# Turning q, k and x by crossbar transposes instead of TensorE in five of eight half batches

## The chip, the cores and the metric

The kernel runs on one core of a Trainium2 chip. Times are device microseconds of one execution; the median of several runs is quoted. A profile is one more execution, with a span a little shorter than the time (233.5 us of 235.3 for the kernel before).

## The reference

Attention with a window of 96 positions, 8 global positions and a linear bias, then a feed-forward layer with a squared ReLU. Shapes: 4 batches, 8 heads, 768 positions, head size 64; model width 512, inner width 2048.

```python
def _attn_ref(q, k, v, n_global, n_local):
    B, H, S, D = q.shape
    scores = np.matmul(q, k.transpose(0, 1, 3, 2)) / np.sqrt(D)
    # keep: key position < n_global, or 0 <= query - key < n_local; bias: -slope[h] * distance
    ...
    a = np.exp(scores - max); a = a / (sum(a) + 1e-09)
    return np.matmul(a, v)

def _moe_ref(x, w_in, w_out):
    h = np.maximum(x @ w_in, 0.0)
    return h * h @ w_out
```

## The kernel before

The work is cut into eight half batches (hb 0 to 7) of 384 rows. While the feed-forward layers of one half batch run on TensorE, the attention of the next is woven in between. Per half batch and pair of heads (four pairs) the attention does this: **turn** q and k (transposes, so that the head size lies on the partitions), **score**, exponential on ScalarE, weighing with a mask on VectorE, **attend** (multiply with v), normalise, and turn the result into **x**, the input of layer 1. Two small copies serve the global positions: `kb` (keys) and `vb` (values, the "fix-up").

```python
def fix_v(x):                                   # the value fix-up
    t0, t1 = tiles_before(x)
    def emit(e):
        v_, vb = x.bt.v, x.bt.vb
        d0, d1 = t0 - 1, t1 - 1
        copy(e, vb[GR:GR * 2, d0:d1], v_[GR:GR * 2, t0:t1])
        copy(e, vb[2 * GR:P, d0:d1], v_[2 * GR:P, t0:t1])
        copy(e, vb[0:GR, d0:d1], v_[0:GR, 0:1].to_broadcast([GR, t1 - t0, H, D + 1]))
    n = t1 - t0
    costs = {"POOL": 0.6 + 2.1 * n} if x.hb > 1 else {"DVE": 0.2 + 0.65 * n}
    x.vb_op = plan.add(costs, emit, x.v_in)

def turn(x, a):                                 # six TensorE transposes, two evacuations, kb
    def emit(e):
        state["ps"] = trp = ps_att.tile([P, 2, HT, P], FP16, name="trp", tag="att")
        for i, st in enumerate((x.sq, x.sk)):
            for t in range(HT):
                nc.tensor.transpose(out=trp[:, i, t, :], in_=st[:, t, 2 * a:2 * a + 2, :],
                                    identity=ident)
    ...
    ops = [evac(0), evac(1)]                    # {"ACT": 0.39, "DVE": 0.31} each
    ...
    x.qk_ops[a] = ops + [plan.add(costs, fix_k, [ops[1]])]

def to_x(x, a):                                 # three transposes, one evacuation
    ...
    job = plan.pe(3 * 0.056, emit, [norm], [att])
    x.x_ops[a] = plan.after(job, {"ACT": 0.39, "DVE": 0.31}, lambda e: copy(
        e, x.xt[:, a, :], st["trx"].rearrange("p t c -> p (t c)")))
```

The order in each engine's queue comes from a schedule computed while the kernel is built: every piece has an estimated cost and a list of what it needs, and goes into its engine's queue where this model says that it can start. On the chip each engine works through its queue in that order, and waits at an instruction whose data are not there (in the changed kernel's profile VectorE stood 2.2 us at one copy in this way). So a piece that the model believes ready too early makes everything behind it wait.

The softmax here doesn't subtract the row's maximum and nothing guards it: scores larger than these inputs give would overflow.

## Time and profile before

| | before |
|---|---|
| time, median of the first 3 runs (range) | 236.13 us (235.42 to 236.17) |
| span of the profile | 233.5 us |
| busy: TensorE, VectorE, ScalarE, GpSimd | 221.1, 126.0, 139.1, 86.2 us |
| half-batch period, mean of five | 26.2 us |

The prediction reads the views that bound the kernel. Here are three groups of instructions from the page of the kernel before that the change removes or moves; the columns are line, engine, operation, destination and source, count, then busy us and mean ns of one, then the idle time before them and who ended it.

```profile
L362 PE MATMUL trp<-ident,sk 128*128 128x128 f16 x84 | 10.0, 226 | 1.5 <-DMA sk<-in_k_dram 1.5
...
L189 ACT COPY qk<-trp 128x384 f16<-128x384 f16 (+1 forms) x43 | 19.9, 506 | 11.4 <-DVE qk L191 10.4
...
L191 POOL COPY vb<-v 32x520 f16<-32x520 f16 (+3 forms) x18 | 19.3, 1070 | 19.1 <-DMA v<-in_v_dram 18.5
```

The second line is an evacuation of turned q or k from PSUM. The third is the value fix-up on GpSimd: about 1 us a copy, and GpSimd waited 18.5 us for v to land before such copies.

### The profile page before, as it was taken

The page shows a single profiled execution, that of the slowest core. Times are in us where ns is not written, and L with a number is a line of the kernel's source. Part 1 is how long each engine was busy: PE and PEld are TensorE (multiplying, and loading weights), DVE is VectorE, ACT ScalarE, POOL GpSimd, SP SyncE. Part 2 cuts the span into 40 slices and gives each one's busy share as a digit, 9 for nine tenths or more (in the row PEclk, how much of TensorE's full clock was granted, in tenths as well). Part 3 has the DMA queues.
Part 4 walks back from the last instruction along what each step waited for, and adds up shares of the span by engine and source line. Part 5 has one row for each costly group of instructions (what it writes and reads, how often), then busy time and mean ns, then how long its engine had stood idle before and what let it go on. Part 6 is the DMA issues. An engine that isn't in the chain of part 4 may idle for free.

```text
span 233.5 us, 5024 instructions
## 1 busy us (share of the span) xinstructions
PE 221.1 (95%) x2023; PEld 133.8 (57%) x2023; DVE 126.0 (54%) x340; ACT 139.1 (60%) x319; POOL 86.2 (37%) x100
## 2 busy tenths in 40 slices
PE   7675999999999999999999999999999999999993
PEld 6553689654555566556655565556655565556541
DVE  5395799441376279425864279325863279323300
ACT  4693797671564598328961598328961598327521
POOL 8948723894457307670292107560000000000000
PEclk9999799999999999999999999999999999999999
DMA  8999999999159907951099107941002100111012
GB/s 149 168 194 155 200 206 193 156 149 108 45 77 164 148 0 50 162 87 46 0 120 171 49 3 51 162 82 45 3 1 93 45 4 0 48 45 45 0 48 90
DMA packets 82583, 20.77 MB, mean 89 GB/s; under 512 B 75392, under 2 KB 79488, under 8 KB 82560
## 3 DMA queue, kind: packets, MB, share of 16 engines
q0 software_dynamic: 74944, 13.11, 74.5%
q1 hardware_dynamic: 6576, 7.08, 9.1%
q10 hardware_dynamic: 1040, 0.26, 0.5%
q8 instruction: 16, 0.26, 0.5%
q14 instruction: 7, 0.06, 0.1%
HBM read 27.26 MB, written 6.29 MB: 144 GB/s over the span
## 4 chain that ended last, share of the span: by engine, by line
PE 88%; POOL 5%; DMA 4%; DVE 0%; issue 0%; ACT 0%; POOLq 0%
PE hps L508 37%; PE yps L556 36%; PE sp L409 5%; PE trp L362 4%; DMA sk<-in_k_dram 4%; PE av L464 4%; PE trx L488 2%; POOL sq L279 2%; POOL v L279 1%; POOL sk L279 1%; POOL w_in_sb L327 1%; ACT y L189 0%; DVE ident L226 0%; DVE qk L191 0%; POOL dist L220 0%
## 5 line engine op out<-in xcount | busy, mean ns | idle before, releaser
L508 PE MATMUL hps<-xt,w_in_sb 128*128 128x384 f16 (+2 forms) x576 | 93.8, 311 | 0.2 <-DMA w_in_sb<-in_moe_w_in_dram 0.2
L556 PE MATMUL yps<-w_out_sb,h 128*128 128x512 f16 x384 | 91.9, 379 | 0.0
L508 PEld LDWEIGHTS <-w_in_sb 128*128 128x128 f16 x576 | 51.4, 99 | 27.7 <-DMA w_in_sb<-in_moe_w_in_dram 0.4
L532 ACT ACTIVATE hr<-hps 128x384 f16<-128x384 f32 (+1 forms) x109 | 56.3, 517 | 12.0 <-PE hps L508 9.8
L543 DVE TENSOR_TENSOR h<-hr 128x768 f16<-128x768 f16 (+1 forms) x68 | 36.8, 541 | 38.0 <-ACT hr L532 36.9
L556 PEld LDWEIGHTS <-h 128*128 128x128 f16 x384 | 34.5, 98 | 33.6
L424 ACT ACTIVATE ex<-sp 128x384 f16<-128x384 f32 x112 | 44.4, 510 | 4.2 <-PE sp L409 4.1
L189 ACT COPY y<-yps 128x512 f32<-128x512 f32 x22 | 12.9, 585 | 55.1 <-PE yps L556 55.1
L279 POOL DMA_DIRECT2D sq<-in_q_dram x23 | 20.8, 914 | 38.0 <-PE trp L362 36.5
L189 ACT COPY qk<-trp 128x384 f16<-128x384 f16 (+1 forms) x43 | 19.9, 506 | 11.4 <-DVE qk L191 10.4
L191 POOL COPY vb<-v 32x520 f16<-32x520 f16 (+3 forms) x18 | 19.3, 1070 | 19.1 <-DMA v<-in_v_dram 18.5
L279 POOL DMA_DIRECT2D v<-in_v_dram x24 | 21.4, 918 | 7.3 <-DMA w_out_sb<-in_moe_w_out_dram 3.3
L279 POOL DMA_DIRECT2D sk<-in_k_dram x21 | 18.6, 908 | 5.9 <-DMA w_out_sb<-in_moe_w_out_dram 3.1
L440 DVE TENSOR_TENSOR phat<-ex,mask 128x768 f16<-128x768 f16 x32 | 16.4, 553 | 5.4 <-ACT ex L424 5.1
L191 DVE COPY qk<-trp 128x384 f16<-128x384 f16 (+1 forms) x19 | 6.9, 365 | 17.5 <-PE trp L362 13.4
L473 DVE TENSOR_TENSOR tm<-av,rec 128x384 f16<-128x384 f32 x28 | 15.6, 557 | 1.0
L464 PEld LDWEIGHTS <-phat 128*128 128x128 f16 x312 | 13.2, 98 | 4.8
L464 PE MATMUL av<-v,phat 128*128 128x65 f16 x192 | 13.2, 193 | 0.0
L436 DVE TENSOR_TENSOR phat<-ex,mask 128x768 f16<-128x768 f16 (+1 forms) x24 | 10.7, 486 | 3.6 <-ACT ex L424 3.5
L464 PE MATMUL av<-vb,phat 128*128 128x65 f16 x120 | 12.1, 193 | 0.0
L191 DVE COPY kb<-qk 128x96 f16<-128x96 f16 (+4 forms) x58 | 10.2, 222 | 3.5 <-ACT qk L189 2.0
L362 PE MATMUL trp<-ident,sk 128*128 128x128 f16 x84 | 10.0, 226 | 1.5 <-DMA sk<-in_k_dram 1.5
(59 smaller groups left out, 154.8 us busy)
## 6 DMA issues: line engine op xcount, KB each, us to landing
out_dram<-y SPq DMA_DIRECT2D x24, 256.0 KB, 2.0
v<-in_v_dram POOLq DMA_DIRECT2D x24, 128.0 KB, 6.3
sq<-in_q_dram POOLq DMA_DIRECT2D x23, 128.0 KB, 5.8
sk<-in_k_dram POOLq DMA_DIRECT2D x21, 128.0 KB, 5.9
w_in_sb<-in_moe_w_in_dram POOLq DMA_DIRECT2D x4, 512.0 KB, 9.0
w_out_sb<-in_moe_w_out_dram POOLq DMA_DIRECT2D x4, 512.0 KB, 14.3
rk<-in_k_dram SPq DMA_DIRECT2D x2, 256.0 KB, 6.2
rk<-in_k_dram ACTq DMA_DIRECT2D x1, 256.0 KB, 4.6
```

What stands on the lines that cost most here:

```text
L189: nc.scalar.copy(out=out, in_=in_)
L191: eng(e).tensor_copy(out=out, in_=in_)
L279: nc.gpsimd.dma_start(out=dst, in_=src[x.b, :, r0 + t * P:r0 + (t + 1) * P, :] .rearrange("h p d -> p h d"))
L362: nc.tensor.transpose(out=trp[:, i, t, :], in_=st[:, t, 2 * a:2 * a + 2, :], identity=ident)
L424: nc.scalar.activation(out=st["ex", g][:, h, 0:n], in_=st[g][h][:, 0:n], func=AF.Exp, scale=scale)
L440: eng(e).tensor_tensor(out=phat[:, :, c0:c0 + n].rearrange("p e (i c) -> p e i c", c=P), in0=ex[:, :, 0:n].rearrange("p e (i c) -> p e i c ...
L464: nc.tensor.matmul(av[:, h, j, :], lhsT=phat[:, h, c * P:(c + 1) * P], rhs=rhs, start=n == 0, stop=n == len(mine) - 1)
L473: nc.vector.tensor_tensor(out=st["tm"].rearrange("p t e d -> p e t d"), in0=av[:, :, :, 0:D], in1=rec[:, :, :, None].to_broadcast([P, 2, H ...
L508: nc.tensor.matmul(st["ps"][:, i * n:(i + 1) * n], lhsT=w_in_sb[:, kk, m * P:(m + 1) * P], rhs=x.xt[:, kk, c0:c1], start=kk == 0, stop=kk ...
L532: nc.scalar.activation(out=o, in_=i, func=AF.Relu)
L543: eng(e).tensor_tensor(out=x.h2[:, m0:m0 + width, c0:c1], in0=hr, in1=hr, op=ALU.mult)
L556: nc.tensor.matmul(st["ps"], lhsT=x.h2[:, m, j * P:(j + 1) * P], rhs=w_out_sb[:, m, :], start=m == 0, stop=m == NFT - 1)
```

## The change

For half batches 3 to 7 q and k are transposed by two DMA transposes (crossbar) from SBUF to SBUF, and x by four. TensorE's transposes and the PSUM evacuations of these half batches go. q and k are turned as soon as loads and the sync queue allow. The value fix-up goes to VectorE, one tile at a time. The layout of `qk` and the places of the attention pieces change to suit. The core, with cuts:

```diff
-        bt.qk = qk_p.tile([P, 2, NPAIR, S], FP16, name="qk", tag="qk")
+        bt.qk = qk_p.tile([P, 2, NT, NPAIR, P], FP16, name="qk", tag="qk")
...
-            return plan.load(0.62, emit, vbefore if name == "v" else before)
+            return plan.load(0.9, emit, vbefore if name == "v" else before)
...
+        x.vb_ops = []
+        for t in range(t0, t1):
+            def emit(e, t=t):
+                copy(e, vb[GR:GR * 2, t - 1], v_[GR:GR * 2, t])
+                copy(e, vb[2 * GR:P, t - 1], v_[2 * GR:P, t])
+                copy(e, vb[0:GR, t - 1], v_[0:GR, 0])
+            x.vb_ops.append(plan.add({"DVE": 0.75}, emit, x.v_in))
...
+    def turn_by_dma(x):
+        ts = slice(x.half * HT, (x.half + 1) * HT)
+        late = list(halves[x.hb - 2].x_ops.values()) if x.hb > 3 else []
+        for i, (name, loads) in enumerate((("sk", x.k_in), ("sq", x.q_in))):
+            def emit(e, i=i, name=name):
+                nc.sync.dma_start_transpose(
+                    out=x.bt.qk[:, 1 - i, ts].rearrange("p t a c -> p (t a) c"),
+                    in_=getattr(x, name).rearrange("p t h d -> p (t h d)"))
+            op = plan.add({"SP": 1.7}, emit, [*loads, x.bt.op, *late])
+            op.lag = 2.5
+            x.turned.append(op)
+        for a in range(NPAIR):
+            x.qk_ops[a] = x.turned + [plan.add(*fix_k(x, a), x.turned[:1])]
...
+    def to_x_by_dma(x, a):
+            nc.sync.dma_start_transpose(
+                out=x.xt[:, a, :].rearrange("p (t c) -> p t c", c=P),
+                in_=st["tm"].rearrange("p t e d -> p (t e d)"))
+        x.x_ops[a] = plan.add({"SP": 1.2}, emit, [norm])
+        x.x_ops[a].lag = 2.5
...
+        early = x.hb > 2
+        for a in range(NPAIR):
+            at = 0.04 + 0.16 * a if early else 0.1 + 0.17 * a
+            jobs.append((at, lambda a=a: score(x, a)))
+            jobs.append((at + 0.17, lambda a=a: attend(x, a)))
+            if early:
+                jobs.append((at + 0.17, lambda a=a: to_x_by_dma(x, a)))
+            else:
+                jobs.append((0.04 * a, lambda a=a: turn(x, a)))
+                jobs.append((at + 0.3, lambda a=a: to_x(x, a)))
```

Six y buffers instead of three, and stores placed by the schedule as pieces of the sync queue, come with it.

More of the change, by code (lines that the diff above doesn't have):

```diff
@@ L176 @@
     h_p = ctx.enter_context(tc.tile_pool(name="hp", bufs=2))
-    y_p = ctx.enter_context(tc.tile_pool(name="yp", bufs=3))
+    y_p = ctx.enter_context(tc.tile_pool(name="yp", bufs=6))
     ps_big = ctx.enter_context(tc.tile_pool(name="ps_big", bufs=6, space=bass.MemoryType.PSUM))
@@ L269, in list_loads @@
         prev = halves[x.hb - 2] if x.hb >= 2 else None
-        before = [prev.turned[-1]] if prev else []
+        before = (prev.turned if prev else []) + (halves[x.hb - 1].turned if x.hb > 3 else [])
         vbefore = [halves[x.hb - x.half - 3].attended[-1]] if x.hb >= 4 else []
@@ L292, in list_loads @@
         else:
-            raw = {n: stage_p.tile([P, HT, H, D], FP32, name=n, tag=n, bufs=1)
-                   for n in ("rq", "rk")}
+            raw = {n: stage_p.tile([P, ts, H, D], FP32, name=n, tag=n, bufs=1)
+                   for n, ts in (("rq", 1), ("rk", HT))}
             x.q_in, x.k_in, x.v_in = [], [], []
@@ L342, in fix_v, with fix_k @@
         t0, t1 = tiles_before(x)
-        def emit(e):
-            v_, vb = x.bt.v, x.bt.vb
-            d0, d1 = t0 - 1, t1 - 1
-            copy(e, vb[GR:GR * 2, d0:d1], v_[GR:GR * 2, t0:t1])
-            copy(e, vb[2 * GR:P, d0:d1], v_[2 * GR:P, t0:t1])
-            copy(e, vb[0:GR, d0:d1], v_[0:GR, 0:1].to_broadcast([GR, t1 - t0, H, D + 1]))
-        n = t1 - t0
-        costs = {"POOL": 0.6 + 2.1 * n} if x.hb > 1 else {"DVE": 0.2 + 0.65 * n}
-        x.vb_op = plan.add(costs, emit, x.v_in)
+        x.vb_ops = []
+        for t in range(t0, t1):
+            def emit(e, t=t):
+                v_, vb = x.bt.v, x.bt.vb
+                copy(e, vb[GR:GR * 2, t - 1], v_[GR:GR * 2, t])
+                copy(e, vb[2 * GR:P, t - 1], v_[2 * GR:P, t])
+                copy(e, vb[0:GR, t - 1], v_[0:GR, 0])
+            x.vb_ops.append(plan.add({"DVE": 0.75}, emit, x.v_in))
+    def fix_k(x, a):
+        t0, t1 = tiles_before(x)
+        def emit(e):
+            kt = x.bt.qk[:, 1, :, a, :]
+            copy(e, x.bt.kb[:, a, t0 - 1:t1 - 1, GR:P], kt[:, t0:t1, GR:P])
+            copy(e, x.bt.kb[:, a, t0 - 1:t1 - 1, 0:GR],
+                 kt[:, 0:1, 0:GR].to_broadcast([P, t1 - t0, GR]))
+        return {"DVE": 0.2 + 0.08 * (t1 - t0)}, emit
     def turn(x, a):
@@ L367, in emit @@
             def emit(e):
-                copy(e, x.bt.qk[:, i, a, x.half * HALF:(x.half + 1) * HALF],
-                     state["ps"][:, i].rearrange("p t c -> p (t c)"))
+                copy(e, x.bt.qk[:, i, x.half * HT:(x.half + 1) * HT, a, :], state["ps"][:, i])
             return plan.after(job, {"ACT": 0.39, "DVE": 0.31}, emit)
         ops = [evac(0), evac(1)]
-        t0, t1 = tiles_before(x)
-        def fix_k(e):
-            kt = x.bt.qk[:, 1, a, :].rearrange("p (t c) -> p t c", c=P)
-            copy(e, x.bt.kb[:, a, t0 - 1:t1 - 1, GR:P], kt[:, t0:t1, GR:P])
-            copy(e, x.bt.kb[:, a, t0 - 1:t1 - 1, 0:GR],
-                 kt[:, 0:1, 0:GR].to_broadcast([P, t1 - t0, GR]))
-        n = t1 - t0
-        costs = {"DVE": 0.2 + 0.08 * n}
-        if x.hb == 0:
-            costs["POOL"] = 0.5 + 0.17 * n
-        x.turned.append(job)
-        x.qk_ops[a] = ops + [plan.add(costs, fix_k, [ops[1]])]
+        x.turned.append(job)
+        x.qk_ops[a] = ops + [plan.add(*fix_k(x, a), [ops[1]])]
+    def turn_by_dma(x):
[11 more added lines that the diff above has]
+            x.qk_ops[a] = x.turned + [plan.add(*fix_k(x, a), x.turned[:1])]
     GROUPS = {
@@ L407, in emit @@
                         lhsT = (bt.kb[rows, a, r - 2, :] if before and r > 1
-                                else bt.qk[rows, 1, a, (r - before) * P:(r - before + 1) * P])
+                                else bt.qk[rows, 1, r - before, a, :])
                         nc.tensor.matmul(pair[h][:, i * P:(i + 1) * P], lhsT=lhsT,
-                                         rhs=bt.qk[rows, 0, a, r * P:(r + 1) * P],
+                                         rhs=bt.qk[rows, 0, r, a, :],
                                          start=True, stop=True)
@@ L465, in emit @@
                                          rhs=rhs, start=n == 0, stop=n == len(mine) - 1)
-        job = plan.pe(0.0305 * 2 * len(where), emit, weighs + [x.vb_op] + x.v_in, [att])
+        job = plan.pe(0.0305 * 2 * len(where), emit, weighs + x.vb_ops + x.v_in, [att])
         def norm(e):
@@ L492, in to_x, with emit @@
             e, x.xt[:, a, :], st["trx"].rearrange("p t c -> p (t c)")))
+    def to_x_by_dma(x, a):
+        st, norm = x.tm[a]
+        def emit(e):
+            if x.xt is None:
+                x.xt = h_p.tile([P, NCT, HALF], FP16, name="xt", tag="xt")
+            nc.sync.dma_start_transpose(
[3 more added lines that the diff above has]
+        x.x_ops[a].lag = 2.5
     def layer1(x, ms, c0=0, c1=HALF, k0=0, k1=NCT):
@@ L567, in evac @@
             def evac(e):
-                y = y_p.tile([P, d_model], FP32, name="y", tag="y")
-                copy(e, y, st["ps"])
-                r0 = x.hb * HALF + j * P
-                nc.sync.dma_start(out=out[r0:r0 + P, :], in_=y)
-            plan.after(job, {"ACT": 0.52, "DVE": 0.63}, evac)
+                st["y"] = y_p.tile([P, d_model], FP32, name="y", tag="y")
+                copy(e, st["y"], st["ps"])
+            r0 = x.hb * HALF + j * P
+            y_op = plan.after(job, {"ACT": 0.52, "DVE": 0.63}, evac)
+            plan.add({"SP": 0.6}, lambda e: nc.sync.dma_start(out=out[r0:r0 + P, :], in_=st["y"]),
+                     [y_op])
     for x in halves:
@@ L590, in turn_tile @@
         job = plan.pe(8 * 0.07, emit, [x.q_in[t], x.k_in[t], ident_op], [big])
-        cols = slice(t * P, (t + 1) * P)
         ops = [plan.after(job, {"ACT": 0.51, "DVE": 0.36}, lambda e, i=i: copy(
-            e, x.bt.qk[:, i, :, cols], st["ps"][:, i])) for i in range(2)]
+            e, x.bt.qk[:, i, t], st["ps"][:, i])) for i in range(2)]
         if t == 1:
@@ L596, in fix_k @@
                 kt = x.bt.qk[:, 1]
-                copy(e, x.bt.kb[:, :, 0, GR:P], kt[:, :, P + GR:2 * P])
-                copy(e, x.bt.kb[:, :, 0, 0:GR], kt[:, :, 0:GR])
+                copy(e, x.bt.kb[:, :, 0, GR:P], kt[:, 1, :, GR:P])
+                copy(e, x.bt.kb[:, :, 0, 0:GR], kt[:, 0, :, 0:GR])
             ops.append(plan.add({"DVE": 0.5, "POOL": 1.2}, fix_k, [ops[1], x.tile_ops[0][1]]))
@@ L614, in emit @@
                     lhsT = (bt.kb[rows, a, t - 2, :] if before and t > 1
-                            else bt.qk[rows, 1, a, (t - before) * P:(t - before + 1) * P])
+                            else bt.qk[rows, 1, t - before, a, :])
                     nc.tensor.matmul(pair[h][:, a, :], lhsT=lhsT,
-                                     rhs=bt.qk[rows, 0, a, t * P:(t + 1) * P],
+                                     rhs=bt.qk[rows, 0, t, a, :],
                                      start=True, stop=True)
@@ L658, in emit @@
                                          rhs=rhs, start=not before, stop=before == kinds[-1])
-        needs = st["weighs"][a0 // 2::2] + [x.v_in[t]] + ([x.vb_op] if t == 2 else [])
+        needs = st["weighs"][a0 // 2::2] + [x.v_in[t]] + (x.vb_ops if t == 2 else [])
         job = plan.pe(4 * len(kinds) * 0.04, emit, needs, [att])
@@ L690, in attention, with merge @@
     def attention(x):
-        jobs = [lambda: fix_v(x)]
-        for a in range(NPAIR + 3):
-            if a < NPAIR:
-                jobs.append(lambda a=a: turn(x, a))
-            if 0 <= a - 1 < NPAIR:
-                jobs.append(lambda a=a - 1: score(x, a))
-            if 0 <= a - 2 < NPAIR:
-                jobs.append(lambda a=a - 2: attend(x, a))
-            if 0 <= a - 3 < NPAIR:
-                jobs.append(lambda a=a - 3: to_x(x, a))
-        return jobs
-    def merge(main, side, start, stop):
-        done = 0
-        for i, f in enumerate(main):
-            if i >= start:
-                want = len(side) if i >= stop else (i - start) * len(side) // (stop - start)
-                while done < want:
-                    side[done]()
-                    done += 1
-            f()
-        for f in side[done:]:
-            f()
+        jobs = []
+        early = x.hb > 2
[8 more added lines that the diff above has]
+                jobs.append((at + 0.3, lambda a=a: to_x(x, a)))
+        return sorted(jobs, key=lambda j: j[0])
+    def merge(main, side):
+        for i, f in enumerate(main):
+            while side and side[0][0] * len(main) <= i:
+                side.pop(0)[1]()
+            f()
+        for _, g in side:
+            g()
     def l1(x, m0=0):
@@ L759 @@
         x = halves[hb]
-        if hb + 1 < NHB:
-            list_loads(halves[hb + 1])
+        for y in halves[2:4] if hb == 1 else halves[hb + 2:hb + 3]:
+            list_loads(y)
+        if hb == 1:
+            fix_v(halves[2])
         main = l2(x0)[6:] + l2(x) if hb == 1 else l1(x) + l2(x)
         side = attention(halves[hb + 1]) if hb + 1 < NHB else []
-        merge(main, side, 1, len(main) - 3)
+        merge(main, side)
+        if hb + 2 < NHB:
+            fix_v(halves[hb + 2])
+            turn_by_dma(halves[hb + 2])
     with tc.manual_schedule():
```

## The prediction

> **What bounds the kernel now.** I read four views in this order: the page's busy table and slices, the chain that ended last, TensorE's timeline in one repeating stretch, and busy time by stage. First the page, cut to its parts 1, 2 and 4:
>
> ```profile
> PE 221.1 (95%) x2023; PEld 133.8 (57%) x2023; DVE 126.0 (54%) x340; ACT 139.1 (60%) x319; POOL 86.2 (37%) x100
> ...
> PE   7675999999999999999999999999999999999993
> ...
> PEclk9999799999999999999999999999999999999999
> DMA  8999999999159907951099107941002100111012
> ...
> PE 88%; POOL 5%; DMA 4%; DVE 0%; issue 0%; ACT 0%; POOLq 0%
> PE hps L508 37%; PE yps L556 36%; PE sp L409 5%; PE trp L362 4%; DMA sk<-in_k_dram 4%; PE av L464 4%; PE trx L488 2%; POOL sq L279 2%; POOL v L279 1%; POOL sk L279 1%; POOL w_in_sb L327 1%; ACT y L189 0%; DVE ident L226 0%; DVE qk L191 0%; POOL dist L220 0%
> ```
>
> One slice is 5.84 us. TensorE is below 9 only in the first four slices (loads), and from there to the last slice it is full at a full clock. The chain says the same: 88% of the end is TensorE, and the two feed-forward layers are 73% of it. Turning q and k (trp) is 4% and turning x (trx) 2%. That is the part that the change can take out, and it lies on the chain, not beside it. A bare "95% busy" would not prove it, because matmuls are pipelined; so I looked at the order of TensorE's work. From its timeline (start, length, what), one piece of a middle half batch:
>
> ```profile
> 106.62 0.33 PE L362 MATMUL trp<-ident,sq 128*128 128x128 f16 x3
> 106.78 0.33 PE L362 MATMUL trp<-ident,sk 128*128 128x128 f16 x3
> 106.95 1.46 PE L508 MATMUL hps<-xt,w_in_sb 128*128 128x384 f16 x8
> ...
> 121.96 0.28 PE L464 MATMUL av<-v,phat 128*128 128x65 f16 x4
> ...
> 123.12 0.33 PE L488 MATMUL trx<-ident,tm 128*128 128x128 f16 x3
> 123.29 1.89 PE L556 MATMUL yps<-w_out_sb,h 128*128 128x512 f16 x8
> ```
>
> The lengths overlap, so I take starts. Six transposes run from 106.62 to 106.95: 0.33 us, or 0.055 to 0.056 each, although one lasts 219 ns alone. Three x transposes take 123.12 to 123.29, 0.17 us. Each start follows the end of the one before: no gaps, nothing to wait for.
>
> Last, busy time in the two stages of a half batch (layer 1 with most of the next attention; layer 2 with the rest):
>
> ```profile
> 104.10:117.90 13.80, 13.80 (x140) 8.78 (x139) 9.40 (x27) 12.41 (x32) 3.12 (x4) 1.00 0.14 26
> 117.90:130.00 12.10, 12.10 (x95) 6.15 (x92) 5.27 (x14) 3.48 (x9) 7.20 (x10) 1.00 1.57 136
> ```
>
> The columns are length, busy PE, PEld, DVE, ACT, POOL, clock, DMA. ScalarE is busy 12.41 of 13.80 us in the first stage: second in line, near its limit there, nearly idle after.
>
> **What the Trainium skill says.** (1) "TensorE: Matmul & The Clock Gate", Part 4: a 128x128 transpose took about 275 ns in one kernel's context. The trace has 219 ns as duration but a spacing of 0.056 us; the spacing is what removal returns. (2) "DMA: Bandwidth & Descriptors", Latency and other measured facts: a crossbar transpose moved 261 GB/s in one kernel. No transposing DMA is in the trace before, so this is unchecked. (3) The same page, "Issuing engines are not separate DMA queues": all DMAs share the same 16 engines. The trace agrees in part: loads issued alike land after a median of 6 us, but the w_out pieces queued together after 14.3 us. (4) "SBUF — State Buffer", SBUF: two separate sides: VectorE in its two-port modes locks GpSimd out, so that descriptors for GpSimd's DMAs are written later. That touches the value fix-up moved to VectorE; no run here shows its size yet.
>
> **The change, part by part.**
>
> TensorE, on the path. Per half batch 24 transposes of q and k and 12 of x go: 36 x 0.0557 = 2.0 us (4 x 0.33 + 4 x 0.17). It holds for half batches 3 to 7, five of seven that use this form; half batch 2 and the opening keep TensorE transposes. 5 x 2.0 = 10.0 us. The chain gives a cross-check: trp plus trx are about 6.3% of 233.5, 14.7 us for seven half batches including the stretched opening, and 5/7 of it is 10.5. I take 10.0. The five half-batch periods run from 77.7 to 208.9 us, 131.2 us or 26.2 each; they should become 24.2 each.
>
> ScalarE and VectorE, beside. Each of those half batches loses 12 evacuations of PSUM. By the groups, over the seven: 40 on ScalarE at 498 ns and 16 on VectorE at 356 for q and k, 8 and 20 for x. Five sevenths: ScalarE loses (18.3+3.9) x 5/7 = 15.9 us, VectorE (5.6+7.0) x 5/7 = 9.0. VectorE gains the value fix-up, 12 tiles of three copies of 520 elements; its own fast copies of that size took 286 ns, so 12 x 3 x 0.286 = 10.3 us. VectorE ends about level, ScalarE lower, GpSimd loses 19.2 us of vb copies (8.9+4.4+4.1+1.8). None of this is on the path. But the scores now come at 0.04, 0.20, 0.36 and 0.52 of the iteration, so all four fall in layer 1, where three did. Layer 1 there has six evacuations fewer for ScalarE (about 2.6 us) and four exponentials more (four in a row took 1.42 us): 12.4 becomes about 11.3 us in a stage of about 13. It stays below TensorE.
>
> DMA, beside if in time. Two transposes of 393 KB for q and k and four of 98 KB for x per half batch. At the skill's 261 GB/s an estimate is 1.5 and 0.4 us of moving; the nearest thing in the trace, storing 256 KB, landed 2.0 us after issue. The kernel's own schedule allows 4.2 us for one of q or k and 3.7 us for one of x. Even 10 us each would fit for q and k, since they are made a whole period of 24 us ahead. The tight one is x of the last pair: its attention is put ahead of the eighth-last piece of layer 2, 8 x 0.864 = 6.9 us before the next layer 1. With the 0.3 us of value matmuls themselves there are 7.2 us, of which about 1.3 pass until the division is done (matmuls, reciprocal 0.20, multiply 0.56, hops). That leaves 5.9 us from issue to landing, against 3.7 allowed: 2.2 us of slack. The loads (nine per half batch, 0.91 us apart on GpSimd, about 8 us) should be over by then.
>
> Stores wait in the same queue; six y buffers instead of three keep ScalarE from being held by them. Opening (to 40 us) and the last half batch (208.9 to 233.5) keep their work.
>
> Sum: 236.1 - 10.0 = 226.1. For imperfect overlap I add 0.7 us: 226.8 us.
>
> **The rivals.** (a) **The last x transpose comes late**, a DMA wait in place of the TensorE transpose, on the path five times. For it: the sync queue is in order, so a q/k transpose that waits for its load, or a store, holds x behind it; a load's latency before was 5.8 to 6.3 us. Against: 2.2 us of slack. If each were 1 us over it costs 5 us: 231. (b) **VectorE or ScalarE becomes the bound in layer 1.** For it: 12.4 of 13.8 us of ScalarE now, a fix-up added, and VectorE's queue is in order too, so a fix-up placed before v has landed stops squares and weights behind it; GpSimd's fix-up waited 18.5 us in sum for v in this profile. Against: evacuations go, and the schedule now counts 0.9 us per load, not 0.62. Half a microsecond per period gives 228.6. (c) **The transposes slow the loads or themselves and the chain of loads to transposes to scores does not fit 24 us.** For it: low-rate transposes would share the 16 engines. Against: about 8 us of loads, perhaps 8 of transposes, so 16 of 24. If it failed, all gain and more would go: 240 or above. (d) **The removed transposes were hidden anyway**, 0 gain: 236. Against: the gapless timeline. I give this little.
>
> **Range and chances.** 226.1 is the floor as long as nothing else moves; the opening's order may shift by half a microsecond either way, so the low end is 225.2. Losses of (a) and (b) together up to some 4 us give a high end of 230.5. Faster by over 2% means under 231.4: 0.88. Within 2%: 0.09, mostly (a) at over a microsecond each. Slower: 0.03, (c).
>
> **What would show it.** Right: in the middle, TensorE without gaps, no trp or trx after half batch 2, periods near 24.2 us, ScalarE down by about 16 us, VectorE level, the chain still over 85% TensorE. Rival (a) shows as a wait of hps (L508 of before) for the DMA that writes xt, at each start of layer 1; (b) as TensorE waits for ScalarE's or VectorE's relu, exponentials or squares, and VectorE waits for the load of v; (c) as scores waiting for a DMA that writes qk, with a DMA share near full. The prediction is wrong if x takes over 6 us from issue to landing, or if the granted clock falls below the 1.00 of these stages now that matmuls are denser.

## The result

The changed kernel took 226.2 us in the median of 4 runs (225.91 to 226.62), the kernel before 235.77 beside it. The ratio is 0.9595, with a 95% interval from 0.9567 to 0.9623: faster by 4.05%. Here and below a ratio is the mean time of one kernel's fast runs over that of the other's in the same rounds, so it is not quite the ratio of the quoted medians. Executions over 1.5% slower than the fastest of the same kernel are left out of the means. The prediction was 226.8, in a range of 225.2 to 230.5.

The page of the changed kernel, the parts that answer to those shown for the kernel before (span, busy time, slices of 5.6 us, chain that ended last):

```profile
span 224.6 us, 4741 instructions
...
PE 211.9 (94%) x1862; PEld 125.1 (56%) x1862; DVE 128.5 (57%) x361; ACT 124.2 (55%) x280; POOL 66.8 (30%) x82
...
PE   7687879999999999999999999999999999999992
...
PEclk9889999999999999999999999999999999999999
DMA  7999999999899995999999721149012111220011
...
PE 79%; DMA 9%; POOL 5%; DVE 5%; ACT 1%; issue 1%; POOLq 0%
PE yps L579 36%; PE hps L531 32%; PE av L475 5%; DMA sk<-in_k_dram 5%; DMA qk<-sk 4%; PE sp L420 4%; POOL sq L279 2%; DVE vb L191 1%; POOL v L279 1%; DVE phat L451 1%; PE trp L370 1%; POOL sk L279 1%; POOL w_in_sb L327 1%; DVE kb L191 1%; PE trx L499 1%
```

TensorE is as full as before and still at full clock in the middle; it simply has 9.2 us less to do, with 161 instructions fewer (180 transposes fewer, and 81 warm-up transposes on zeros, which fill TensorE's waits in the opening, where it had 62). The chain now has turning at 1% each where it had 4% and 2%. A new member is a DMA, `qk<-sk` at 4%, though its chain share overstates it; see below. The DMA row changed too: from 58 to 129 us, where the kernel before has slices of 0, 1 and 5, all slices but one are now at 7 or more.

Busy time by stage in one middle period of the changed kernel, layer 1 and layer 2 (length, busy PE, PEld, DVE, ACT, POOL, clock, DMA, GB/s):

```profile
103.10:116.50 13.40, 13.40 (x136) 8.03 (x135) 10.09 (x29) 11.63 (x30) 7.88 (x9) 1.00 1.64 147
116.50:127.10 10.60, 10.60 (x60) 5.00 (x58) 3.53 (x10) 1.58 (x4) 0.00 (x0) 1.00 1.05 131
```

The period is 24.0 us where it was 25.9, TensorE has no gap, and ScalarE is busy 11.63 us of layer 1's 13.40 instead of 12.41 of 13.80.

From the changed kernel's groups and DMA issues: the fix-up on VectorE, and the issue-to-landing medians of the transposes.

```profile
L191 DVE COPY vb<-v 32x520 f16<-32x520 f16 (+1 forms) x48 | 17.8, 372 | 0.8
...
xt<-tm SPq DMA_TRANSPOSE x20, 2.3
...
qk<-sq SPq DMA_TRANSPOSE x5, 5.5
qk<-sk SPq DMA_TRANSPOSE x5, 4.5
```

And two of the waits in the changed kernel (who waited for whom: us in total, times, longest):

```profile
DVE kb L191 <- DMA qk<-sk: 2.2, 1, 2.2
...
PE av L475 <- DVE phat L451: 0.3, 1, 0.3
```

VectorE stood still once for 2.2 us at `kb`, behind a transpose of keys that landed 9.6 us after its issue (the longest of the ten), and TensorE waited 0.3 us as a consequence. That single spot is where the chain jumps to the DMA. Note that these keys were not needed for another 19 us: the landing was at 85.2, and the attention that reads them began at 104.4. VectorE waited because `kb` stood next in its queue. It is a small crack here. The experiments show what lies under it.

**Where the time went.** Layer 1 of half batch 2 starts at 77.60 us before and 78.35 after; layer 1 of half batch 7 at 208.91 and 199.94. So the opening lost 0.75 us, five periods gained 9.7, and the rest is unchanged.

### The profile page after: what moved, and what is told of

It reads as the page before. It is cut to its first block, busy times and chain, and to the rows that moved or that the text cites. A ratio compares the mean times of both kernels' runs of the same rounds, so it can differ in the third digit from the quotient of the medians.

```text
span 224.6 us, 4741 instructions
## 1 busy us (share of the span) xinstructions
PE 211.9 (94%) x1862; PEld 125.1 (56%) x1862; DVE 128.5 (57%) x361; ACT 124.2 (55%) x280; POOL 66.8 (30%) x82
## 4 chain that ended last, share of the span: by engine, by line
PE 79%; DMA 9%; POOL 5%; DVE 5%; ACT 1%; issue 1%; POOLq 0%
PE yps L579 36%; PE hps L531 32%; PE av L475 5%; DMA sk<-in_k_dram 5%; DMA qk<-sk 4%; PE sp L420 4%; POOL sq L279 2%; DVE vb L191 1%; POOL v L279 1%; DVE phat L451 1%; PE trp L370 1%; POOL sk L279 1%; POOL w_in_sb L327 1%; DVE kb L191 1%; PE trx L499 1%
## 5 line engine op out<-in xcount | busy, mean ns | idle before, releaser
L531 PE MATMUL hps<-xt,w_in_sb 128*128 128x384 f16 (+2 forms) x576 | 89.5, 308 | 1.5 <-DMA w_in_sb<-in_moe_w_in_dram 1.3
L579 PE MATMUL yps<-w_out_sb,h 128*128 128x512 f16 x384 | 86.5, 379 | 0.0
L566 DVE TENSOR_TENSOR h<-hr 128x768 f16<-128x768 f16 (+1 forms) x68 | 35.5, 530 | 52.2 <-ACT hr L555 52.1
L555 ACT ACTIVATE hr<-hps 128x384 f16<-128x384 f32 (+1 forms) x107 | 53.7, 508 | 16.2 <-PE hps L531 14.4
L579 PEld LDWEIGHTS <-h 128*128 128x128 f16 x384 | 36.6, 98 | 41.4
L189 ACT COPY y<-yps 128x512 f32<-128x512 f32 x23 | 13.5, 586 | 63.3 <-PE yps L579 63.3
L279 POOL DMA_DIRECT2D sq<-in_q_dram x23 | 20.4, 899 | 30.7 <-DMA qk<-sq 28.3
L191 DVE COPY vb<-v 32x520 f16<-32x520 f16 (+1 forms) x48 | 17.8, 372 | 0.8
L475 PEld LDWEIGHTS <-phat 128*128 128x128 f16 x312 | 11.8, 97 | 4.5 <-DVE phat L451 0.8
L475 PE MATMUL av<-v,phat 128*128 128x65 f16 x192 | 13.5, 194 | 0.3 <-DVE phat L451 0.3
L189 ACT COPY qk<-trp 128x384 f16<-128x384 f16 (+1 forms) x13 | 6.5, 529 | 9.9 <-DVE qk L191 9.0
L482 DVE RECIPROCAL rec<-av 128x6 f32<-128x6 f32 x28 | 5.4, 194 | 8.8 <-PE av L475 8.7
L420 PE MATMUL sp<-qk 64*128 64x128 f16 x192 | 10.4, 219 | 0.0
```

The lines of the kernel that those rows point to most:

```text
L189: nc.scalar.copy(out=out, in_=in_)
L191: eng(e).tensor_copy(out=out, in_=in_)
L279: nc.gpsimd.dma_start(out=dst, in_=src[x.b, :, r0 + t * P:r0 + (t + 1) * P, :] .rearrange("h p d -> p h d"))
L420: nc.tensor.matmul(pair[h][:, i * P:(i + 1) * P], lhsT=lhsT, rhs=bt.qk[rows, 0, r, a, :], start=True, stop=True)
L475: nc.tensor.matmul(av[:, h, j, :], lhsT=phat[:, h, c * P:(c + 1) * P], rhs=rhs, start=n == 0, stop=n == len(mine) - 1)
L531: nc.tensor.matmul(st["ps"][:, i * n:(i + 1) * n], lhsT=w_in_sb[:, kk, m * P:(m + 1) * P], rhs=x.xt[:, kk, c0:c1], start=kk == 0, stop=kk ...
```

## The experiments

The theory: TensorE's transposes are the gain, because it was full without gaps. Rivals: the 60 evacuations taken from ScalarE and VectorE are the gain; the new order or GpSimd's relief is; and, for what stayed hidden, that the load-to-transpose chain is close to full. Twelve kernels ran, each giving correct results. All edits are to the changed kernel.

| run | us, median of all runs | ratio to before (95% interval) | expected, us |
|---|---|---|---|
| changed kernel | 226.2 | 0.9595 (0.9567 to 0.9623) | 226.8 |
| e1_no_crossbar | 236.25 | 1.0019 (0.9995 to 1.0043) | 235.5 to 237.0 |
| e2_x_on_pe | 229.49 | 0.9736 (0.9712 to 0.9760) | 229.5 |
| e3_qk_on_pe | 234.38 | 0.9975 (0.9910 to 1.0040) | 232.9 |
| e4_pe_work_back | 236.63 | 1.0036 (1.0012 to 1.0060) | 236.2 |
| e5_evacuations_back | 231.30 | 0.9794 (0.9765 to 0.9822) | 226 to 227.2 |
| e6_opening_fixup_whole | 226.56 | 0.9602 (0.9584 to 0.9621) | 225.5 |
| e7_fixup_on_pool | 237.10 | 0.9956 (0.9929 to 0.9982) | 225.5 |
| e10_turn_twice | 246.65 | 1.0456 (1.0421 to 1.0491) | 226 to 227.2 |
| e13_evac_back_late_kb | 227.53 | 0.9646 (0.9620 to 0.9671) | 226 to 228 |
| e14_pool_fixup_late_kb | 231.02 | 0.9779 (0.9742 to 0.9816) | 226 to 229 |
| e15_turn_twice_late_kb | 238.93 | 1.0094 (1.0045 to 1.0142) | 226 to 231 |
| e17_best | 236.42 | 1.0009 (0.9972 to 1.0046) | 224.3 |

The last column is the theory's expectation (theory B where there are two). Slow runs, by the 1.5% mark, are in three rows (two of four runs in e7_fixup_on_pool, one of four in e15_turn_twice_late_kb, one of six in e17_best); the ratios leave them out, and so does the text below, where the mean of the fast runs is used for these three. The changed kernel ran only in the first session. The experiments ran in three later ones, on chips 2, 7 and 3, where the median of the kernel before was 235.9 to 236.2 us instead of 235.77, so differences of some 0.4 us to the changed kernel mean nothing. The first four runs confirm the theory; e5, e6, e7 and e10 were misses and led further.

### Taking the crossbar away, whole and in parts

**e1_no_crossbar**

```diff
-        early = x.hb > 2
+        early = False
...
             fix_v(halves[hb + 2])
-            turn_by_dma(halves[hb + 2])
```

> All of the change but the crossbar: the new layout of qk, the value fix-up on VectorE, six y buffers, the new places of the attention pieces; q, k and x are turned on TensorE everywhere. Theory (TensorE's transposes are the whole gain): within 1 us of the kernel before, 235.5 to 237.0, since 36 transposes per half batch are back; about 0.8 us above rather than below, because of the opening. Rival (the gain is from the new order or from GpSimd's relief): 226 to 231.

Measured: 236.25 us, 0.2% above before, with 0.24% of uncertainty either way. So layout, order, buffers and the fix-up on VectorE are together worth nothing by themselves. (Here and in e3 the condition for the loads of q and k is as in the kernel before, which the cuts leave out.) The opening behaves as in the changed kernel, a little worse: layer 1 of half batch 2 starts at 79.13 us, of which 0.34 are six transposes now put ahead of it.

**e2_x_on_pe**

```diff
-                jobs.append((at + 0.17, lambda a=a: to_x_by_dma(x, a)))
+                jobs.append((at + 0.3, lambda a=a: to_x(x, a)))
```

> The changed kernel with x of half batches 3 to 7 back on TensorE (12 transposes and 4 evacuations per half batch). Theory: 5 x 4 x 0.17 = 3.3 us slower than the changed kernel, about 229.5. Rival (x by crossbar was hidden and worth nothing, or its latency costs what it saves): 226.2 or less.

Measured: 229.49 us, 3.3 us above the changed kernel, as expected to the tenth.

**e3_qk_on_pe**

```diff
+            if early:
+                jobs.append((0.04 * a - 0.02, lambda a=a: turn(x, a)))
             at = 0.04 + 0.16 * a if early else 0.1 + 0.17 * a
...
-            turn_by_dma(halves[hb + 2])
```

> The changed kernel with q and k of half batches 3 to 7 back on TensorE, x still by crossbar (24 transposes and 8 evacuations per half batch back). Theory: 5 x 4 x 0.33 = 6.7 us slower than the changed kernel, about 232.9; more if the transposes' evacuations crowd ScalarE in layer 1. Rival: under 230.

Measured: 234.38 us, but the four runs spread from 233.44 to 236.85. The fastest is 7.2 us above the changed kernel, near the 6.7 expected; the median is 8.2 above. In the profile (of the run at 233.44) TensorE waited 0.7 us for a square. What the slower runs waited for is not in any profile, so the extra 1.5 us stay open. The direction is as the theory has it.

### TensorE's work back, or the evacuations back

**e4_pe_work_back**: six matmuls ahead of each pair's scores and three ahead of its values, on zeros; the real matmuls overwrite their results.

```diff
+                    for _ in range(6 if x.hb > 2 else 0):
+                        nc.tensor.matmul(pair[0][:, 0:P], lhsT=zero[:, 0:P], rhs=zero[:, 0:P],
+                                         start=True, stop=True)
...
+            for _ in range(3 if x.hb > 2 else 0):
+                nc.tensor.matmul(av.rearrange("p e t d -> p (e t d)")[:, 0:P], lhsT=zero[:, 0:P],
+                                 rhs=zero[:, 0:P], start=True, stop=True)
```

> The changed kernel plus 9 matmuls of 128 columns per pair (36 per half batch 3 to 7) whose results are overwritten: TensorE's time comes back, the evacuations of PSUM do not. Theory (TensorE's time alone): 36 x 0.056 x 5 = 10.0 us slower than the changed kernel, about 236.2. Rival (the 60 evacuations that left ScalarE and VectorE made the gain): 226 to 229.

Measured: 236.63 us. Putting 180 short matmuls back on TensorE (and their time into the schedule's estimates), and nothing else, takes back the whole gain and 0.4 us more. The crossbar transposes still ran in this kernel and ScalarE's evacuations were still gone. This settles where the gain is.

**e5_evacuations_back**: three copies per pair of the attended values from PSUM into a scratch tile that nothing reads.

```diff
+        for i in range(3 if x.hb > 2 else 0):
+            def spill(e):
+                nc_out = scratch[e]
+                copy(e, nc_out, st["av"].rearrange("p e t d -> p (e t d)")[:, 0:3 * P])
+            plan.after(job, {"ACT": 0.39, "DVE": 0.45}, spill)
```

> The changed kernel plus 12 copies of 128x384 from PSUM per half batch 3 to 7 on ScalarE or VectorE, whose results nothing reads: the evacuations come back, TensorE's work does not. Theory (evacuations lie beside TensorE): within 1 us of the changed kernel, 226 to 227.2. Rival (ScalarE and VectorE were what held the kernel): most of the 10 us back, 231 or more.

Measured: 231.30 us, a miss: 5.1 us where I expected at most one. Taken alone this would support the rival that ScalarE is nearly binding. But this kernel's waits show something else as well; VectorE stood still three times at `kb`:

```profile
DVE kb L191 <- DMA qk<-sk: 4.3, 3, 1.7
```

**e13_evac_back_late_kb** tells the two apart. The copies stay, but `kb` is put later in VectorE's queue: behind the seventh of twelve layer 2 pieces of the iteration before use, instead of where the schedule believes that the transpose has landed.

```diff
-            x.qk_ops[a] = x.turned + [plan.add(*fix_k(x, a), x.turned[:1])]
+            x.qk_ops[a] = x.turned + [plan.add(
+                *fix_k(x, a), x.turned[:1] + halves[x.hb - 2].l2jobs[6:7] +
+                (halves[x.hb - 1].qk_ops[a] if x.half else []))]
```

(`l2jobs` is a list of the layer 2 pieces. The last term keeps the order right where half a batch depends on its first half.)

> The run with 12 unread evacuations per half batch (it cost 5 us), but the copies of k for the global columns (kb) stand later in VectorE's queue: behind the seventh of twelve layer 2 pieces of the iteration before use, instead of where the schedule believes the crossbar transpose has landed. Theory B (VectorE's in-order queue stood still at kb behind a late DMA, and that made the loss): 226 to 228. Theory A (ScalarE is crowded in layer 1): still 230 to 231.5.

Measured: 227.53 us, theory B. In its waits there is no wait of VectorE for `qk<-sk` any more. ScalarE is busy 140.9 us in this profile, more than in the kernel before (139.1), and the kernel is still 3.5% faster than that one. So the evacuations cost about 1.3 us against the changed kernel, and the other 3.8 went with the place of a copy that nobody needed yet. Moving `kb` alone, without the extra copies, was not run; if it gains the 0.3 us of the stall seen in the changed kernel, the evacuations cost 1.6.

### Is the transposes' DMA time hidden?

**e10_turn_twice**: each q and k transpose issued twice into the same place. The second waits for the first to land, so both the DMA work and the latency of a turn double.

```diff
+                for _ in range(2):
                     nc.sync.dma_start_transpose(...)
...
-            op = plan.add({"SP": 1.7}, emit, [*loads, x.bt.op, *late])
+            op = plan.add({"SP": 3.4}, emit, [*loads, x.bt.op, *late])
```

> The changed kernel with every crossbar transpose of q and k issued twice (the same result twice). Theory (made a half batch ahead, their DMA time is hidden): within 1 us of the changed kernel, 226 to 227.2. Rival (loads, transposes and scores form a chain that is nearly full): 5 us or more slower.

Measured: 246.65 us, 20 us above the changed kernel: a clear miss. The second transpose did wait for the first (the sync queue stood 37.4 us at these in sum). Its waits:

```profile
DVE kb L191 <- DMA qk<-sk: 19.0, 4, 9.7
...
PE av L476 <- DVE phat L448: 13.5, 2, 8.8
```

VectorE stood still 19.0 us at `kb`, up to 9.7 at a time, and TensorE waited 13.5 us for weighings that stood behind it in VectorE's queue. After its gaps TensorE also ran slower: the granted clock was 0.74 from 60 to 80 us and 0.83 from 120 to 140, and the same 1862 instructions were busy 4.7 us longer than in the changed kernel. In its sync queue one pair of transposes holds the queue for 8 us and more, with the x transposes behind it:

```profile
86.86 8.48 SPq L389 DMA_TRANSPOSE qk<-sk  x2
```

**e15_turn_twice_late_kb** is the same with `kb` placed late, by the edit shown above.

> The run with every q and k transpose issued twice (it cost 20 us), with kb later in VectorE's queue as above. Theory B (there is DMA time enough, only VectorE's place in the queue was wrong): 226 to 231, the x transposes behind the doubled ones may cost a few us. Theory A (load, transpose, score is a full chain): 240 or more.

Measured: 238.1 us in the mean of the three fast runs (236.52, 238.69, 239.17). It lies between the two theories: 8.5 of the 20.4 us come back, the rest does not. The profile fell in the run that counts as slow (240.14), so I take its waits only as a lead:

```profile
DVE vb L191 <- DMA v<-in_v_dram: 7.9, 1, 7.9
...
PE trx L502 <- DVE tm L487: 8.2, 1, 8.2
```

VectorE now stands still at the next copy of its kind, the value fix-up, whose loads were held up behind the doubled transposes (a load of q may overwrite its buffer only after the transpose has read it; GpSimd waited 48.6 us for that here, 28.3 in the changed kernel). The chain of load, transpose and next load seems to have less room than I thought, between 60 and 100 us above all, where the loads of one half batch follow on another's. How much of the 11.9 us left is this queue order and how much is lack of DMA time is not settled.

### The value fix-up

**e6_opening_fixup_whole**: half batches 0 and 1 with three copies over all tiles again, in place of three per tile.

```diff
+        if x.hb < 2:
+            def whole(e):
+                (the three copies of the kernel before)
+            n = t1 - t0
+            costs = {"POOL": 0.6 + 2.1 * n} if x.hb > 1 else {"DVE": 0.2 + 0.65 * n}
+            x.vb_ops.append(plan.add(costs, whole, x.v_in))
+            return
```

> The changed kernel with the value fix-up of half batches 0 and 1 again as three copies over all tiles. In the opening of the changed kernel nine copies on VectorE (3.4 us) stand ahead of the first weighing on the chain; TensorE begins its gapless stretch 0.8 us later than before. Theory: 0.5 to 0.8 us of that come back, 225.5. Rival (the 0.8 us is the wait for w_in or the clock): 226.2.

Measured: 226.56 us, not different from the changed kernel. In its profile layer 1 of half batch 2 starts at 77.93 instead of 78.35 us, so 0.42 of the 0.75 us came back there, but runs vary by as much, and the times do not show it. Inconclusive. TensorE waits 1.5 us for pieces of w_in in this profile too (1.3 in the changed kernel's), and only 0.2 in the profile before, where a clock of 0.57 from 24 to 28 us delayed TensorE by then instead.

**e7_fixup_on_pool**: the fix-up of all half batches as in the kernel before, on GpSimd from half batch 2 on. (Here too the order of `kb` needed the dependency on the first half, else VectorE would have read keys not yet written.)

```diff
+        if True:
+            def whole(e):
+                (the three copies of the kernel before)
+            n = t1 - t0
+            costs = {"POOL": 0.6 + 2.1 * n} if x.hb > 1 else {"DVE": 0.2 + 0.65 * n}
+            x.vb_ops.append(plan.add(costs, whole, x.v_in))
+            return
```

> The changed kernel with the whole value fix-up as before: GpSimd from half batch 2 on (and the opening as in the run with the whole fix-up). Theory (the fix-up's engine lies beside the path): as the run with the opening's fix-up whole, 225.5, within 0.7. Rival (the fix-up on VectorE was needed for the gain, since GpSimd's copies hold back its loads for the crossbar): 227.5 or more.

Measured: 234.8 us in the mean of the two fast runs (234.59 and 235.1), another miss: without the fix-up's move 8.6 us of the gain are lost, although the prediction put the fix-up beside the path. Its timeline of VectorE, of GpSimd and of TensorE in the same five microseconds, one after the other:

```profile
93.71 3.43 DVE L463 TENSOR_TENSOR phat<-ex,mask 128x768 f16<-128x768 f16 x2
```

```profile
93.49 4.99 POOL L191 COPY vb<-v 32x1560 f16<-32x1560 f16 x3 [9.54 <-DMA v<-in_v_dram]
```

```profile
95.44 0.20 PE L487 MATMUL av<-v,phat 128*128 128x65 f16 x1 [0.48 <-DVE phat L463]
97.19 0.20 PE L487 MATMUL av<-vb,phat 128*128 128x65 f16 x1 [1.56 <-DVE phat L463]
```

Two weighings took 3.43 us where two take about 1.0 elsewhere in this profile: a single one took up to 1.84 us instead of 0.55, while GpSimd copied. TensorE waited 1.56 us for one of them, and 3.4 us for weighings in the whole profile. (Another 2.7 us were waits for evacuated q and k of half batch 2 near 62 and 66 us; the first comes right after VectorE had stood 1.86 us at `kb`.) In the kernel before, the same three GpSimd copies are nearly as long, but fell elsewhere:

```profile
100.20 4.52 POOL L191 COPY vb<-v 32x1560 f16<-32x1560 f16 x3 [3.16 <-DMA v<-in_v_dram]
```

That is the end of layer 2 (layer 1 follows at 104.0), where VectorE has little to do. VectorE also waited 7.2 us at `kb` in the e7 profile, since GpSimd issued its loads later: its queue is in order too, and it stood at the fix-up 21.6 us for v, with the next loads behind.

**e14_pool_fixup_late_kb** takes the waits at `kb` away and leaves the copies on GpSimd.

> The run with the value fix-up on GpSimd (it lost the whole gain, 237), with kb later in VectorE's queue as in the run above. Theory B (loads held up by GpSimd's copies make the transposes late, and VectorE stands still at kb): 226 to 229. Theory A (the scores or values themselves come too late because of GpSimd): 233 or more.

Measured: 231.0 us: 3.8 of the 8.6 us come back, so more than theory A has and less than B. What is left shows in its profile: in VectorE's timeline the same overlap, in TensorE's another victim of it, then busy time of the stretches around it (columns as above, the clock third from the end):

```profile
93.02 2.86 DVE L464 TENSOR_TENSOR phat<-ex,mask 128x768 f16<-128x768 f16 x2
```

```profile
97.69 0.60 PE L592 MATMUL yps<-w_out_sb,h 128*128 128x512 f16 x2 [2.20 <-DVE h L579]
```

```profile
90.00:100.00 10.00, 7.80 (x67) 3.87 (x66) 8.38 (x19) 3.24 (x8) 7.68 (x7) 0.95 0.73 56
100.00:110.00 10.00, 10.00 (x53) 4.60 (x52) 1.53 (x6) 3.07 (x8) 5.06 (x6) 0.88 2.18 155
```

TensorE waited 2.20 us for a square (h) that stood behind the stretched weighings, and the granted clock was 0.95 and 0.88 in the mean of the two stretches of ten microseconds that hold and follow the gap, by my estimate a further loss of 10 x 0.05 + 10 x 0.12 = 1.7 us. Two more waits of TensorE in this profile, 0.6 us before a value matmul near 64 us and 1.1 us for x near 132 us, bring the sum to 5.6, close to the 5.4 us by which its span exceeds the changed kernel's. The overlap with GpSimd, with the slower clock after its gap, is thus seen for about 4 us of it; what caused the two smaller waits was not followed up.

### A kernel that might be better still

**e17_best**: `kb` late, q and k of half batch 2 by crossbar too, and x of its first two pairs.

```diff
             fix_v(halves[2])
+            turn_by_dma(halves[2])
...
-                jobs.append((0.04 * a, lambda a=a: turn(x, a)))
-                jobs.append((at + 0.3, lambda a=a: to_x(x, a)))
+                if x.hb < 2:
+                    jobs.append((0.04 * a, lambda a=a: turn(x, a)))
+                if a < 2:
+                    jobs.append((at + 0.17, lambda a=a: to_x_by_dma(x, a)))
+                else:
+                    jobs.append((at + 0.3, lambda a=a: to_x(x, a)))
```

> An attempt at a better kernel: the changed kernel with kb later in VectorE's queue, q and k of half batch 2 by crossbar too, and the first two of its x transposes. If TensorE's time is what counts: 4 x 0.33 + 2 x 0.17 = 1.7 us less, and up to 0.3 us from VectorE, so about 224.3. Rival (from 40 to 75 us the DMA engines are full with loads, two more transposes make later ones late): 226 or more.

Measured: 236.1 us in the mean of the five fast runs, the rival. Two of VectorE's waits in its profile:

```profile
DVE kb L191 <- DMA qk<-sk: 7.6, 1, 7.6
DVE vb L191 <- DMA v<-in_v_dram: 6.1, 1, 6.1
```

From 40 to 80 us the DMA engines are busy with loads; the loads and transposes that follow the one more turn came late, and VectorE stands still at `kb` (of half batch 2, which this edit does not delay) and at the fix-up. So the edit did not try its own remedy at the place that stalled; a late `kb` there was not run. No version that ran beats the changed kernel.

## Why the prediction was right

**TensorE's sum** was right. It said 5 x 2.0 = 10.0 us; the five periods gained 9.7, x alone is worth 3.3 (e2, predicted 3.3), and giving the time back without the evacuations costs 10.4 (e4). The choice that carried it was to price a transpose by its spacing (0.056 us), not by its duration (219 ns, which would have said 39 us), and to show that the timeline had no gaps.

**The allowance of 0.7 us** was about right in size, by luck: it was meant for imperfect overlap, and went to the opening (0.75 us) and to one stall (0.3 us), not to late x transposes. x landed 2.3 us after issue in the median, against 3.7 allowed, but the longest of the twenty took 6.2, which is over the 6 us that the prediction had named as a sign of being wrong. It was one of the first three pairs of its half batch, which have more time; the last pair, the tight one, took at most 4.3, and no TensorE wait for x is in the changed kernel's waits. The stages stayed at a clock of 1.00. The low end of the range, 225.2, is not the sum that its sentence gives (226.1 less 0.5 is 225.6).

**ScalarE down by 16 us, VectorE level**: ScalarE fell by 14.9 (139.1 to 124.2), VectorE rose by 2.5. The copy of the fix-up took 372 ns in the mean instead of 286: the prediction priced all copies as 32 partitions of 520 elements, but a third of them have 64 partitions, and in the kernel before such a copy took 564 ns. GpSimd fell by 19.4, as said. Layer 1's ScalarE time was put at 11.3 us and is 11.63.

**Chain over 85% TensorE** was wrong: 79%. The chain runs through the keys' transpose at the one place where VectorE stood still, and that wait cost TensorE 0.3 us, not the 4% of the span that the chain shows. A share of the chain is not a saving. Two readings of the profile before were loose as well, without harm to the sum: the fifth slice is not at full clock (its digit is 7), and the w_out pieces whose landing took 14.3 us are 512 KB against the loads' 128, so they show little about sharing.

**The weakest steps** did not hurt the number, but the runs show them to be wrong. "None of this is on the path", said of the evacuations and the fix-up, holds for the evacuations only as long as no one else delays VectorE (e5, e13), and the fix-up left on GpSimd costs 8.6 of the 9.6 us (e7). "Even 10 us each would fit for q and k" is false: doubled transposes cost 20 us (e10). The step that failed is the reckoning of slack by need, a whole period ahead. VectorE's queue does not know the need; it holds `kb` where the schedule expected the landing, 1.7 us of issue and 2.5 us after, and the landings were 3.8 to 9.6 us after issue. Rival (b) named this danger, but for the load of v, not for `kb`, and gave it half a microsecond per period. Rival (c), that the transposes slow the loads, is there in a small way: q, k and v landed after a median of 6.7 to 6.8 us, where they took 5.8 to 6.3 before. Whether sharing the DMA engines or the fix-up on VectorE did this was not separated.

## What to carry to other kernels

Where an engine is full without gaps, the spacing of the removed instructions times their count is the gain, and a run that puts only that engine's time back tests it. When work moves to a DMA, put the first instruction that waits for it as late in its engine's in-order queue as its reader allows; a transfer far ahead of its need still stalls whoever waits for it early. In this kernel a copy on GpSimd was beside the path only where VectorE had little to do: check where it will fall after the change, not where it fell before.

## What the Trainium skill lacked or had wrong

- "SBUF — State Buffer", SBUF: two separate sides, says that VectorE and GpSimd share a port pair under an exclusive lock, which also counts for a VectorE instruction with two SBUF inputs against a GpSimd one that reads SBUF, such as a weighing against a fix-up copy. The runs agree, and add the size: a weighing of 128x768 took up to 1.84 us instead of 0.55 beside a GpSimd copy, and TensorE waited 1.56 us for one of them (e7).
- "TensorE: Matmul & The Clock Gate", Part 4: PE-mode transpose, gives about 275 ns in one kernel's context. Here one took 219 ns, and back to back they were 0.056 us apart; Part 4 lacks that spacing for transposes (Part 1 has it for ordinary matmuls of this size), and it is what a removal returned here.
- "DMA: Bandwidth & Descriptors", Latency and other measured facts, gives 261 GB/s for transposes in one kernel, but no time from issue to landing; the page "VectorE: DVE Perf Modes", The three transpose paths, has 1309 ns for a single 128x128 block only. Here 98 KB landed after a median of 2.3 us, and 393 KB after 3.8 to 9.6 us beside loads. At 261 GB/s an estimate for 393 KB is 1.5 us of moving, so the rate alone would have misled here.
- None of the pages that I used says what a DMA wait early in an in-order VectorE queue costs: 5.1 us against 1.3 over the changed kernel in a pair of runs (e5, e13) that differ in the place of `kb` alone, up to the order noted there.
